# First loads in another queue order, and a new order of the work, in a fused attention and gated-FFN kernel

## The chip, the cores and the metric

The kernel runs on one core of a Trainium2 chip. The metric is the device time of one execution in microseconds (us): 387.93 us is the median of three runs of the kernel before (386.91 to 388.13).

## The reference, cut to what matters

```python
def phi(x):
    proj = np.einsum('bhsd,df->bhsf', x, w_phi)
    proj = proj - np.max(np.abs(proj), axis=-1, keepdims=True)
    return np.concatenate([np.exp(proj), np.exp(-proj)], axis=-1)
q_p, k_p = (phi(q), phi(k))
kv = np.einsum('bhsf,bhsd->bhfd', k_p, v)
z = np.sum(k_p, axis=2)
num = np.einsum('bhsf,bhfd->bhsd', q_p, kv)
den = np.einsum('bhsf,bhf->bhs', q_p, z)[..., None] + 1e-06
attn = num / den                      # 8 batches, 8 heads, 576 tokens, head size 64
x = attn.transpose(0, 2, 1, 3).reshape(4608, 512)
gate = np.maximum(x @ w_gate, 0.0)    # 512 x 1536
out = (gate * (x @ w_val)) @ w_out    # 1536 x 512
```

All inputs are float32. The kernel takes its matmuls in bf16.

## The kernel before, in words

Attention of eight batches feeds nine groups of a gated FFN. Of the 576 tokens of a batch, 512 are worked on as four chunks of 128; the other 64 are the "tails", which are taken together for two batches. FFN group g takes the 512 main tokens of batch g, and group 8 takes the tails of all batches.

The work is cut into small pieces, "atoms", each a few instructions on one or two engines, with a key. For batch b they are:

- k side, for each pair of heads u: `kT` (TensorE, PE in the profile, turns k by four transposing matmuls; batches 0 and 1 only, the others are turned by DMA), `kTc` (copy out of PSUM), `kr` (projection, L310), `km` (row maxima on VectorE, DVE, L317), `ke` (exponentials on ScalarE, ACT, L366), `kk` (factors `ek`, L377), `vs` (v times the factors, on GpSimd, POOL, or DVE, L326), `kv` (product of features and v, L447) and `kvc` (its copy, L455). Atoms with `u` in the key and `vsm` do the same for the tails.
- q side, for each half cp of the chunks: `qT` and `qTc` (turned as k is, eight transposes, L269 and L282), `qc` and `qr` (projections both ways), `qe` (exponentials, L504), `qm` (row maxima), `qk`, then `n` (numerators, L534), `nt` and `nu` (DVE, L553 and L565), `xu` (division, L574), and `xT` with `xc` (turning of the result, L269 and L594) or `xd` (the same by DMA).
- FFN group g: `fv` (value product and its copy by ACT or DVE, L665 and L680), `fg` (gate product and the DVE operation that joins both, L687) for 12 slices of 128 columns, and `fo` (output product, L713, copy, L723, store). Group 0 begins with 8 steps of half width (256 tokens), so that it can start when the first two chunks are there, and goes on with 8 of full width.

Nothing schedules these atoms at run time. The string `ORDER` lists their numbers, and `atoms.run` emits them in that order, so every engine's instruction stream and every DMA queue follows it; an engine executes its stream strictly in order. A prime behind a number puts that atom's copy or product on the other of two engines. `z5` emits five dummy matmuls on zeros (`keep_busy`, L193). PSUM is handed out in eight banks in turn.

Ahead of `ORDER` stand the first loads of batch 0, in float32: `w_phi` to `wf`, cast on DVE to `w2` (the profile's `w`); k into the buffer `vn1`, v into `vn0`; the tails into `km` and `vm`. POOL then copies one element of a loaded tile to `gate`, which holds back the loads behind it in POOL's stream (`ld` atoms: q, k of later batches and the weights, cast to bf16 on the way). v of later batches is loaded on SyncE's (SP's) queue.

## Time and profile before

| | |
|---|---|
| median of 3 runs | 387.93 us |
| the profiled execution's own time | 389.6 us |
| its span, first to last instruction | 387.8 us |
| PE busy | 368.0 us (95%) |
| DVE busy | 296.1 us (76%) |
| ACT busy | 217.9 us (56%) |
| POOL busy | 141.4 us (36%) |
| moved by DMA | 45.13 MB, mean 116 GB/s |

All times in the profile are counted from the start of the span. "Busy" is the time in which an engine executes something; the idle time before an instruction is put down to what released it. The granted clock is TensorE's own, as a share of full speed. A busy PE need not be at its peak, since ends of matmuls are modelled.

### The profile page before, as it was taken

The numbers are of one execution on the slowest core, as the hardware profiler recorded it, in microseconds if no ns is written. First come the engines' busy times: TensorE is split into PE (matmuls) and PEld (weight loads), VectorE is DVE, ScalarE is ACT, GpSimd is POOL, SyncE is SP. The second block draws the span as 40 slices with busy tenths as digits, with TensorE's granted clock in tenths as the row PEclk, the third lists the DMA queues.
The fourth block names the chain that finished last, engine by engine and source line by source line (L and its number), as shares of the span: only waits on it lengthen the run. The fifth ranks groups of instructions, "written<-read, shape, count | busy, mean of one in ns | idle before, by whom it ended". The sixth has DMA issues, their size and how long they took to land.

```text
span 387.8 us, 8651 instructions
## 1 busy us (share of the span) xinstructions
PE 368.0 (95%) x3316; PEld 198.1 (51%) x3365; DVE 296.1 (76%) x640; ACT 217.9 (56%) x509; POOL 141.4 (36%) x186
## 2 busy tenths in 40 slices
PE   4977999999999999999999999999999999999994
PEld 2556646544655555455546454555545544444441
DVE  2995987898898898999958998989777916932630
ACT  1994876569878835994694469664673112103110
POOL 2994383419288236181543235732210210000000
PEclk9998999999999999999999999999999999999999
DMA  7999995997859999993489716920310220011013
GB/s 180 210 239 187 175 179 87 181 210 98 136 83 135 181 189 139 189 203 57 141 158 234 125 41 128 159 56 2 96 54 2 43 96 27 15 54 54 2 27 82
DMA packets 91931, 45.13 MB, mean 116 GB/s; under 512 B 57970, under 2 KB 87282, under 8 KB 91890
## 3 DMA queue, kind: packets, MB, share of 16 engines
q1 hardware_dynamic: 62226, 30.22, 33.0%
q0 software_dynamic: 28256, 13.57, 31.9%
q10 hardware_dynamic: 1408, 0.79, 0.7%
q8 instruction: 26, 0.43, 0.5%
q14 instruction: 15, 0.12, 0.1%
HBM read 37.81 MB, written 9.44 MB: 122 GB/s over the span
## 4 chain that ended last, share of the span: by engine, by line
PE 85%; DMA 5%; DVE 4%; issue 2%; ACT 2%; POOL 1%; ACTq 0%; DVEq 0%; POOLq 0%
PE pa L665 46%; PE pa L713 23%; PE pa L534 5%; PE pa L447 5%; PE pa L310 4%; DMA qn<-in_q_dram 3%; PE pa L486 2%; DMA km<-in_k_dram 2%; PE pa L269 1%; ACT kp L366 1%; DVE mq L317 1%; DVE u L565 1%; DVE t L553 1%; DVE vs L423 0%; POOL vs L326 0%
## 5 line engine op out<-in xcount | busy, mean ns | idle before, releaser
L687 DVE SCALAR_TENSOR_TENSOR h<-pa,val_sb 128x512 bf16<-128x512 f32 (+1 forms) x112 | 74.1, 668 | 37.2 <-PE pa L665 29.0
L665 PE MATMUL pa<-xT,wg_sb 128*128 128x512 bf16 (+1 forms) x384 | 98.0, 371 | 1.2 <-DVE h L687 0.3
L665 PE MATMUL pa<-xT,wv_sb 128*128 128x512 bf16 (+1 forms) x386 | 98.0, 372 | 0.6
L713 PE MATMUL pa<-wo_sb,h 128*128 128x512 bf16 x415 | 97.0, 379 | 0.8 <-issue 0.2
L366 ACT ACTIVATE kp<-pa 128x512 bf16<-128x512 f32 (+1 forms) x148 | 76.9, 609 | 12.3 <-PE pa L310 8.7
L504 ACT ACTIVATE qp<-pa 128x512 bf16<-128x512 f32 x144 | 76.3, 631 | 12.3 <-PE pa L486 12.3
L680 ACT CAST val_sb<-pa 128x512 bf16<-128x512 f32 (+1 forms) x65 | 37.7, 580 | 72.6 <-PE pa L665 67.4
L326 POOL TENSOR_TENSOR vs<-vn,ek 128x512 bf16<-128x512 f32 x56 | 59.5, 1071 | 48.0 <-ACT ek L377 37.3
L574 POOL TENSOR_TENSOR xu<-u,r 128x512 bf16<-128x512 f32 x30 | 31.4, 1049 | 115.0 <-DVE r L572 79.4
L665 PEld LDWEIGHTS <-wv_sb 128*128 128x128 bf16 x448 | 42.0, 98 | 45.0 <-issue 0.7
L665 PEld LDWEIGHTS <-wg_sb 128*128 128x128 bf16 x448 | 41.9, 98 | 44.1 <-issue 0.7
L713 PEld LDWEIGHTS <-h 128*128 128x128 bf16 x432 | 39.8, 98 | 44.7 <-issue 1.2
L317 DVE TENSOR_REDUCE mk<-pa 128x4 f32<-128x512 f32 (+1 forms) x74 | 47.2, 667 | 6.0 <-PE pa L310 5.2
L317 DVE TENSOR_REDUCE mq<-pa 128x4 f32<-128x512 f32 x72 | 45.9, 681 | 4.0 <-PE pa L310 3.9
L553 DVE TENSOR_TENSOR t<-pa,cq 128x195 f32<-128x195 f32 (+3 forms) x120 | 38.1, 328 | 7.3 <-PE pa L534 4.8
L723 ACT COPY out_sb<-pa 128x512 f32<-128x512 f32 x26 | 15.6, 600 | 47.2 <-PE pa L713 40.9
L565 DVE TENSOR_TENSOR u<-pa,t 128x195 f32<-128x195 f32 (+3 forms) x120 | 38.4, 334 | 3.6
L534 PEld LDWEIGHTS <-qp 128*128 128x128 bf16 x640 | 28.5, 98 | 14.2 <-issue 1.7
L680 DVE CAST val_sb<-pa 128x512 bf16<-128x512 f32 (+1 forms) x47 | 31.1, 662 | 4.3 <-PE pa L665 3.5
L534 PE MATMUL pa<-kv,qp 128*128 128x65 bf16 x640 | 31.2, 194 | 1.1 <-ACT qp L504 0.9
L447 PEld LDWEIGHTS <-kp 128*128 128x128 bf16 x640 | 21.7, 97 | 5.5 <-ACT qp L504 0.9
L447 PE MATMUL pa<-vs,kp 128*128 128x65 bf16 x512 | 23.0, 193 | 1.3 <-ACT kp L366 0.5
(69 smaller groups left out, 266.8 us busy)
## 6 DMA issues: line engine op xcount, KB each, us to landing
out_dram<-out_sb SPq DMA_DIRECT2D x32, 256.0 KB, 2.5
vn<-in_v_dram SPq DMA_DIRECT2D x7, 1024.0 KB, 6.7
qn<-in_q_dram POOLq DMA_DIRECT2D x8, 512.0 KB, 8.2
kn<-in_k_dram POOLq DMA_DIRECT2D x7, 512.0 KB, 9.4
wv_sb<-in_moe_w_val_dram POOLq DMA_DIRECT2D x3, 512.0 KB, 10.9
wg_sb<-in_moe_w_gate_dram POOLq DMA_DIRECT2D x3, 512.0 KB, 12.2
...
vn<-in_k_dram SPq DMA_DIRECT2D x4, 256.0 KB, 5.1
```

The lines of the kernel that those rows point to most:

```text
L317: nc.vector.tensor_reduce(m, some.rearrange("p (c f) -> p c f", f=F), axis=AX.X, op=ALU.max, apply_absolute_value=True,)
L326: eng.tensor_tensor(dst[:, :, s, 0:D], src, ek[:, :, s : s + 1].to_broadcast(list(src.shape)), op=ALU.mult,)
L366: nc.scalar.activation(st["kp"][:, s, 0 : n // 2, par, :], st["banks"][par][:, 0 : n // 2 * F].rearrange("p (a f) -> p a f", f=F), AF.Exp, ...
L447: nc.tensor.matmul(kv_ps[:, hh, s, :], lhsT=lhsT, rhs=rhs, start=(n == 0), stop=(n == 19))
L504: nc.scalar.activation(x["qp"][:, s, slot].rearrange("p a b -> p (a b)"), st["cols", i][par], AF.Exp, scale=sign,)
L534: nc.tensor.matmul(pn[:, E * (2 * i + s) : E * (2 * i + s + 1)], lhsT=x["qp"][:, s, slot, blk, :], rhs=kvs[b, (lo + i) // 2][:, (lo + i) % ...
L553: nc.vector.tensor_tensor(x["t", j][rows, 0:n], ab[:, :, 1], c[:, :, None].to_broadcast([np_, n, E]), op=ALU.mult,)
L565: nc.vector.tensor_tensor(x["u"][rows, lo : lo + n], ab[:, :, 0], x["t", j][rows, 0:n], op=ALU.add)
L665: nc.tensor.matmul(ps, lhsT=w[:, dc, P * fi : P * fi + P], rhs=xTs[g][:, dc, lo:hi], start=(dc == 0), stop=(dc == NDC - 1),)
L680: copy_by(copy_of(alt, "ACT", "DVE"))(st["val", n], ps)
L687: nc.vector.scalar_tensor_tensor(st["h2"][:, fi, lo:hi], ps, 0.0, st["val", n], op0=ALU.max, op1=ALU.mult)
L713: nc.tensor.matmul(po, lhsT=st["h2"][:, fi, P * t : P * t + P], rhs=wo_sb[:, fi, c0:c1], start=(fi == 0), stop=(fi == NFC - 1),)
```

## The change

First the loads. Before, SP's queue took `w_phi`, k and v of two heads at a time, and ACT's queue the four tail loads. Now ACT's queue takes `w_phi` alone, and everything else goes to SP: k and v of heads 0 to 3 in turn, then k's tails, k of heads 4 to 7 in one DMA, v's tails, v of heads 4 to 7 in one DMA. The gate reads k of head 2 and no longer k's tails.

```diff
-    def heads_of(u):
-        return slice(2 * u, 2 * u + 2)
-
-    def load_first(name, src, eng, u):
-        load_main(0, name, src, eng, FP32, heads_of(u), buf="vn1" if name == "kn" else "vn0")
-
+    def load_first(name, src, lo, hi):
+        buf = "vn1" if name == "kn" else "vn0"
+        load_main(0, name, src, nc.sync, FP32, slice(lo, hi), buf=buf)
+
+    nc.scalar.dma_start(out=wf, in_=w_phi[None].to_broadcast([2, D, F]))
     inputs["kn", 0] = sb_in.tile([P, H, C, D], FP32, name="vn1")
-    nc.sync.dma_start(out=wf, in_=w_phi[None].to_broadcast([2, D, F]))
-    load_tails("km", k, 0, nc.scalar, FP32)
-    load_tails("vm", v, 0, nc.scalar, FP32)
-    load_first("kn", k, nc.sync, 0)
-    load_first("kn", k, nc.sync, 1)
-    load_first("vn", v, nc.sync, 0)
-    load_first("kn", k, nc.sync, 2)
-    load_first("vn", v, nc.sync, 1)
-    load_first("kn", k, nc.sync, 3)
-    load_first("vn", v, nc.sync, 2)
-    load_first("vn", v, nc.sync, 3)
+    load_first("kn", k, 0, 2)
+    load_first("vn", v, 0, 2)
+    load_first("kn", k, 2, 4)
+    load_first("vn", v, 2, 4)
+    load_tails("km", k, 0, nc.sync, FP32)
+    load_first("kn", k, 4, H)
+    load_tails("vm", v, 0, nc.sync, FP32)
+    load_first("vn", v, 4, H)
...
-    nc.gpsimd.tensor_copy(gate, inputs["km", 0][:, 0, 0:1])
+    nc.gpsimd.tensor_copy(gate, inputs["kn", 0][:, 2, 0, 0:1])
```

Then the whole `ORDER` is a new one, 13 dummy matmuls instead of 9 among it. Of its 62 lines, the first of each:

```diff
-ORDER = """z5 60 7 61' 104 62 64 65 8 116 105' 66 63 0 106 117 67 109 108 118 119 122 128 1 107 111 129 z2 130
...
+ORDER = """z5 104 105' z1 106 108 116 7 109 110 0 60 8 1 117 118 107 61 121 62 z2 128 140 63 111 113 112 120
...
```

By its key, the old one begins with `kT` of the tails (60) and loads q (7) and k of batch 1 (8) before the first weights (0); the new one begins with `kT` of heads 0 and 1 (104), and puts the first weights between q and k of batch 1.

SP's queue before, from its first row (`vn_104` holds k, `vn_114` v of batch 0; the last two rows are v of batch 1's tails and rows):

```order
L737 DMA wf<-in_w_phi_dram 128x1x128
L207 DMA vn_104<-in_k_dram 128x2x256 x2
L207 DMA vn_114<-in_v_dram 128x2x256
L207 DMA vn_104<-in_k_dram 128x2x256
L207 DMA vn_114<-in_v_dram 128x2x256
L207 DMA vn_104<-in_k_dram 128x2x256
L207 DMA vn_114<-in_v_dram 128x2x256 x2
L224 DMA vm<-in_v_dram 64x4x64 x2
L207 DMA vn_531<-in_v_dram 128x8x256
```

And now (`vn_105` holds k, `vn_107` v of batch 0):

```order
L207 DMA vn_105<-in_k_dram 128x2x256
L207 DMA vn_107<-in_v_dram 128x2x256
L207 DMA vn_105<-in_k_dram 128x2x256
L207 DMA vn_107<-in_v_dram 128x2x256
L224 DMA km_111<-in_k_dram 64x4x64 x2
L207 DMA vn_105<-in_k_dram 128x4x256
L224 DMA vm<-in_v_dram 64x4x64 x2
L207 DMA vn_107<-in_v_dram 128x4x256
L224 DMA vm<-in_v_dram 64x4x64 x2
L207 DMA vn_386<-in_v_dram 128x8x256
```

k's first rows now lead the queue, and the tails of k stand behind 1 MB of it.

DVE's stream before, from its first reduction to the copies of the turned q of batch 0 (`mk` are row maxima of k, 128x2 for the tails; the `tT` of 128x1024 are q):

```order
L317 TENSOR_REDUCE mk<-pa 128x2 x2
L282 COPY tT_184<-pa 128x512
L317 TENSOR_REDUCE mk<-pa 128x4 x3
L282 COPY tT_219<-pa 128x512
L317 TENSOR_REDUCE mk<-pa 128x4 x3
L282 COPY tT_265<-pa 128x512
L317 TENSOR_REDUCE mk<-pa 128x4 x2
L282 COPY tT_308<-pa 128x1024
L282 COPY tT_333<-pa 128x1024
```

And now:

```order
L317 TENSOR_REDUCE mk<-pa 128x4
L282 COPY tT_176<-pa 128x512
L317 TENSOR_REDUCE mk<-pa 128x4
L282 COPY tT_189<-pa 128x256
L317 TENSOR_REDUCE mk<-pa 128x4
L317 TENSOR_REDUCE mk<-pa 128x2
L317 TENSOR_REDUCE mk<-pa 128x4
L317 TENSOR_REDUCE mk<-pa 128x2
L282 COPY tT_239<-pa 128x512
L326 TENSOR_TENSOR vs<-vn_107,ek 128x8x64
L317 TENSOR_REDUCE mk<-pa 128x4 x4
L282 COPY tT_307<-pa 128x1024
```

One `vs` product (L326) has come to DVE, the copy of the tails (`tT_189`) too, and one copy of 128x512 has left it for ACT.

PE's stream before, from the turning of the first result chunk to the first FFN matmul (`xu` is the result, `qn` and `kn` are q and k of batch 1, L534 are numerators; the weight loads and repetitions are left out):

```order
L269 MATMUL pa<-ident_98,xu 128x128
...
L269 MATMUL pa<-ident_98,qn 128x128
...
L269 MATMUL pa<-ident_98,kn 128x128
...
L269 MATMUL pa<-ident_98,xu 128x128
...
L534 MATMUL pa<-kv,qp 128x65
...
L269 MATMUL pa<-ident_98,qn 128x128
...
L534 MATMUL pa<-kv,qp 128x65
...
L665 MATMUL pa<-xT,wv_sb 128x256
```

And now:

```order
L269 MATMUL pa<-ident_98,xu 128x128
...
L534 MATMUL pa<-kv,qp 128x65
...
L269 MATMUL pa<-ident_98,xu 128x128
...
L269 MATMUL pa<-ident_98,qn 128x128
...
L534 MATMUL pa<-kv,qp 128x65
...
L665 MATMUL pa<-xT,wv_sb 128x256
```

The first transpose of q of batch 1 used to stand ahead of four transposes of k, the turning of the second result chunk and ten numerator matmuls; now only the other eight transposes of q and four numerator matmuls stand between it and the FFN.

97 lines of the change are left out of this document (46 added, 51 removed), and 25 rows, old and new, of the table ORDER.

## Prediction

> **What bounds the kernel now.** I read the busy times first: PE is busy for 95% of the span. So the time is PE's work plus the gaps before and in it, and the next view is busy time by stretches (PE, PEld, DVE, ACT, POOL, then granted clock, DMA share, GB/s).
>
> ```profile
> 10.00:20.00 10.00, 8.92 (x101) 5.48 (x99) 9.18 (x16) 9.88 (x30) 9.25 (x16) 1.00 1.25 207
> 20.00:30.00 10.00, 7.72 (x160) 6.12 (x160) 9.29 (x28) 9.76 (x24) 9.66 (x14) 1.00 1.24 239
> 35.00:387.80 352.80, 343.71 (x3007) 181.25 (x3053) 273.02 (x585) 194.42 (x451) 118.41 (x148) 1.00 0.62 107
> 80.00:90.00 10.00, 9.37 (x75) 4.54 (x75) 9.45 (x19) 7.86 (x21) 4.42 (x6) 1.00 0.82 188
> 240.00:250.00 10.00, 9.50 (x116) 5.38 (x115) 9.63 (x19) 6.85 (x16) 8.96 (x12) 1.00 0.90 116
> 280.00:290.00 10.00, 9.49 (x100) 4.91 (x97) 7.54 (x14) 8.12 (x21) 1.09 (x1) 1.00 0.14 54
> 380.00:387.80 7.80, 2.77 (x13) 1.08 (x11) 0.69 (x1) 0.58 (x1) 0.00 (x0) 1.00 0.31 87
> ```
>
> From 35 us on PE lacks 352.80 - 343.71 = 9.1 us. Of these 5.0 lie at the very end (7.80 - 2.77: last copy and store, which the change leaves), 1.6 in the three stretches with a real gap, 2.4 in crumbs of some 0.1 in 10 us. A new order can win there 1.6 us at most, and lose as it pleases. From 10 to 30 us it is ACT, DVE and POOL that are full, and DMA moves over 200 GB/s. What ends this front is told by the chain of waits (start, length, what) and by PE's timeline.
>
> ```profile
> 1.49 5.92 DMA km<-in_k_dram
> 19.20 13.03 DMA qn<-in_q_dram
> ```
>
> ```profile
> 29.75 0.39 PE L269 MATMUL pa<-ident,xu 128*128 128x128 bf16 x4
> 32.28 0.62 PE L269 MATMUL pa<-ident,qn 128*128 128x128 bf16 x8 [2.14 <-DMA qn<-in_q_dram]
> 32.73 0.53 PE L269 MATMUL pa<-ident,kn 128*128 128x128 bf16 x4
> 33.06 0.63 PE L269 MATMUL pa<-ident,xu 128*128 128x128 bf16 x4
> 33.48 0.42 PE L534 MATMUL pa<-kv,qp 128*128 128x65 bf16 x4
> 33.72 1.04 PE L269 MATMUL pa<-ident,qn 128*128 128x128 bf16 x8
> 34.56 0.54 PE L534 MATMUL pa<-kv,qp 128*128 128x65 bf16 x6
> 34.91 1.04 PE L665 MATMUL pa<-xT,wv_sb 128*128 128x256 bf16 x4
> 36.43 0.60 PE L665 MATMUL pa<-xT,wv_sb 128*128 128x256 bf16 x4
> ```
>
> PE stands for 2.14 us until q of batch 1 lands, 13.0 us after its issue, and the FFN starts 2.63 us behind that landing (34.91 - 32.28). The stall costs more than itself: the last two rows are the same four matmuls, 1.04 and then 0.60. Stretches of 3.41 us show why:
>
> ```profile
> 26.11:29.52 3.41, 2.31 (x47) 1.80 (x46) 2.96 (x14) 3.40 (x7) 3.09 (x4) 1.00 1.26 254
> 29.52:32.94 3.42, 1.28 (x24) 1.08 (x22) 1.48 (x5) 1.07 (x2) 0.87 (x2) 0.98 1.24 209
> 32.94:36.35 3.41, 3.41 (x34) 3.03 (x32) 1.92 (x7) 1.96 (x4) 1.08 (x2) 0.51 1.38 201
> ```
>
> After a stretch with 1.28 us of matmuls the granted clock is 0.51 for 3.41 us; after one with 2.31 it stayed full. The point at which it falls lies between the two.
>
> **The change part by part.** *First loads.* Today k of heads 0 and 1 is issued at 1.51 and lands at 6.9 (1.51 + 5.4); the k tails release PE near 7.4 (1.49 + 5.92 in the chain).
>
> ```profile
> vn<-in_k_dram SPq DMA_DIRECT2D x1, 256.0 KB, 5.4
> 1.51 0.95 SPq L207 DMA_DIRECT2D vn<-in_k_dram  x2
> 2.00:3.00 1.00, 1.00 (x4) 0.15 (x1) 0.75 (x2) 0.00 (x0) 0.00 (x0) 1.00 0.26 64
> 3.00:4.00 1.00, 0.30 (x1) 0.00 (x0) 0.30 (x1) 0.29 (x1) 0.00 (x0) 1.00 0.91 262
> 4.00:5.00 1.00, 0.00 (x0) 0.00 (x0) 0.00 (x0) 0.99 (x1) 0.00 (x0) 1.00 1.14 213
> 5.00:6.00 1.00, 0.00 (x0) 0.00 (x0) 0.00 (x0) 0.00 (x0) 0.00 (x0) 1.00 1.14 258
> 7.55 0.19 POOL L754 COPY gate<-km 128x1 f32<-128x1 f32 x1 [5.90 <-DMA km<-in_k_dram]
> SPq L207 <- DMA km<-in_k_dram: 2.7, 1, 2.7
> ```
>
> Ahead of that k landing stand `w_phi`, k tails, most of the v tails and k itself, about 576 KB, which by these rows had been moved at 5.2; the landing is 1.7 later. Now only `w_phi` and k are ahead, 320 KB, moved at 4.0: I estimate a landing at 5.8. PE's first real work begins 1.7 us sooner. But the k tails now follow 1.2 MB: 2.6 + 1.2 MB at 240 GB/s + 1.7 = 9.4, and in the new order the projection of heads 2 and 3 stands behind their turning on PE. The gate opens with k of heads 2 and 3, estimated at 7.9, about where it opened (7.55). SP's queue waited 2.7 us for an earlier load before its fifth issue, so the new queue may pause too; 1 MB stands ahead there, which hides it.
>
> *Front work.* DVE's first reduction stood at 9.45; with k landed at 5.8 and 2.5 for turning, copy and projection (the tails took 2.0 from 7.4 to 9.45, and are half as wide) it stands near 8.3. Up to the copies of q, DVE gains a `vs` product (0.89) and the tails' copy (0.3, under half of a 128x512 one) and loses a copy of 0.69. Five dummies come ahead of q's transposes.
>
> ```profile
> 9.45 0.42 DVE L317 TENSOR_REDUCE mk<-pa 128x2 f32<-128x256 f32 x1 [3.16 <-PE pa L310]
> 18.05 1.28 DVE L282 COPY tT<-pa 128x1024 bf16<-128x1024 bf16 x2
> L326 DVE TENSOR_TENSOR vs<-vn,ek 128x512 bf16<-128x512 f32 x8 | 7.1, 891 | 1.4 <-ACT ek L377 1.3
> L282 DVE CAST tT<-pa 128x512 bf16<-128x512 f32 x3 | 2.1, 685 | 0.0
> 0.98 2.32 PE L193 MATMUL pa<-zeros 128*128 128x512 bf16 x5 [0.98 <-DVE zeros L748]
> 16.74 1.07 PE L269 MATMUL pa<-ident,qn 128*128 128x128 bf16 x16
> ```
>
> Five dummies cost 2.32 at half clock, and their cover is DVE, which reaches q's copies at 18.05 today and, by these gains and losses, at about the same time then. If PE is still at half clock there, the cover falls short by about 1 us. So the front's compute comes out between 1.1 early and 1.5 late; I take 0.5 late. Today compute stands ready at 30.1, 2.1 before q lands, so this is hidden.
>
> *q of batch 1.* On POOL's queue it is still the fifth of five 512 KB loads, behind q, first weights and k in another order; v of batch 1 follows on SP as before. DMA is full from 3 us to its landing, the bytes ahead are the same, so I leave it at 32.28, with 31.3 and 33.3 as bounds (the gate or that v up to 1 us apart). k of batch 1 goes behind one more 512 KB load, but its transposes now stand behind the last kv product of batch 0 and three numerator groups: hidden.
>
> *Behind q.* Four transposes of k, the four of the second result and one group of six numerators now stand ahead of the wait. Behind it: 16 transposes and four numerators. At full clock that is 1.07 (the row at 16.74) + 0.2 (half of the 0.42 at half clock) = 1.3 instead of 2.63: 1.4 us gained. Whether the clock is full: the stretch ahead of the landing then holds 1.28 plus these 14 matmuls (some 0.6 us at full clock) plus whatever the front comes late, so 1.9 to 2.9 where 1.28 was too little and 2.31 enough. I take full. Then the FFN work that ran from 34.91 to 36.35 at half clock gains 0.7 more. Together -2.1. The Trainium skill ("TensorE: Matmul & The Clock Gate", What's actually happening) has the clock fall after an idle window of about 3.4 us; here it fell after a window that held 1.28 us of work, so the trace is harsher. By the page's rule it would not fall in the changed kernel either, and the sum stays -2.1.
>
> *The rest of the order.* Value copies on DVE go from 47 to 39, output copies there from 10 to 13; both engines have time (DVE 273 of 353 us). I book +0.6 for the late front and for gaps of a new order, bounds -1.6 (all three gaps gone) and +1.7 (the second rival's extra work).
>
> Sum: -2.1 + 0.6 = -1.5. The profiled execution's own time of 389.6 (span 387.8, 1.8 around it) would be 388.1. It lies 1.67 above the median of the runs, so the median goes from 387.93 to **386.4**.
>
> **The rivals.**
>
> *The clock falls again.* The wait stays and the stretch before it stays too thin. Then the 14 matmuls gain only what they are worth at full clock, 0.55 us, and with 0.3 for the order the time is 387.7. For it: the two bounds leave the point open. Of the Trainium skill's same page, PE-mode transpose says that transposes do not count as PE-busy in the same way; eight of the 14 are transposes, so by it the stretch gains little and this rival wins. The trace gives some support: 3.24 us of matmuls from 9.04 to 12.46, many of them transposes, and the two dummies behind still take 0.5 each, as the five on the cold start did.
>
> ```profile
> 9.04:12.46 3.42, 3.24 (x29) 2.19 (x29) 2.65 (x5) 3.04 (x10) 3.35 (x6) 1.00 0.93 251
> 12.66 1.06 PE L193 MATMUL pa<-zeros 128*128 128x512 bf16 x2
> ```
>
> *DVE becomes the bound in group 0 (slower).* From the FFN's start to group 1, I count on DVE, new against old: two kv copies (0.42 each), a `vs` product (0.89), a q copy of 128x1024 (0.64 by the row at 18.05), a result copy and one `nu` (taken at 0.4 each) more; three value copies (two of half width, 0.4 each, one whole, 0.69) fewer: +1.7 us.
>
> ```profile
> L455 DVE CAST kv<-pa 128x260 bf16<-128x260 f32 x13 | 5.5, 421 | 1.3 <-PE pa L447 1.3
> L680 DVE CAST val_sb<-pa 128x512 bf16<-128x512 f32 x43 | 29.4, 685 | 4.3 <-PE pa L665 3.5
> 40.00:80.00 40.00, 39.63 (x417) 23.26 (x423) 34.74 (x80) 26.76 (x68) 18.11 (x26) 1.00 0.94 157
> ```
>
> DVE was busy 34.74 of 40 there. If PE starts earlier and at full clock, DVE has less time ahead of it and more to do; if it cannot use its free 5.3 us, the -2.1 is given back and the 1.7 come on top: 389.6. It decides when DVE is above 9.7 in 10 us from 35 to 75. Against it: those 5.3 us, and eight PSUM banks that let PE run ahead.
>
> *The loads do not land sooner.* All DMAs share the engines; if k lands at 6.9 as now while its tails land at 9.4 or later, the front is another 1.1 us late. With the 1.5 of its late bound and 0.6 for the 14 matmuls it ends 3.2 behind 30.1, which is 1.0 past q's landing: 387.4.
>
> **How the numbers follow.** Forecast (386.4, its own range 385.0 to 387.5) 0.40; clock falls (387.7) 0.20; DVE or another late engine (389.6) 0.32; late loads (387.4) 0.08. The range goes down to 384.7, the forecast with half the bounded gain in the later gaps and q 1 us sooner, and up to 389.9 to hold the slower case's middle. A measurement of this kernel tells 0.3% (1.2 us) from no change: faster means below 386.8, slower above 389.1. Faster: 0.36 of the forecast's 0.40 and 0.05 of the second case, 0.41. Slower: 0.26 of the third and 0.01 of the fourth, 0.27. The rest, 0.32, lies within.
>
> **What would show it.** Right: k's first transposes near 5.8; no stretch at half clock after 32; the first FFN matmul at 33.2 to 34; PE idle for 9 us or so in all from there on. Wrong in the front: that matmul later than 34.9, with q's landing past 33.3, or q's transposes waited for by ACT or DVE and not by DMA. Wrong in the order: waits of PE for DVE `h` or for `vs` above 0.5 us that are not there now. It would be wrong as a whole if compute, not q of batch 1, is what PE waits for at 32 us.

## The result and the profile after

The changed kernel takes 384.28 us (median of 20 runs, 383.72 to 388.33) against 387.56 us for the kernel before (20 runs, 386.17 to 390.45): ratio 0.9926, interval 0.9906 to 0.9946. That is 3.3 us faster, where 386.4 was predicted and 384.7 was the range's low end. The direction was right and the size was not. (The 387.93 us that the forecast started from is the median of the first three of the 20 runs of the kernel before.)

The profiled execution of the changed kernel took 387.17 us (span 385.4) and is one of its longer ones. A second profile of the same kernel, first experiment below, took 384.48 (span 382.7) and lies at the median, so both are read.

PE's timeline in the first profile (start, length, what, and in brackets the idle time ahead and what ended it): the first transposes of k, the first projection, then the end of the front.

```profile
3.63 1.09 PE L269 MATMUL pa<-ident,vn 128*128 128x128 f32 x4 [0.33 <-DMA vn<-in_k_dram]
6.28 0.40 PE L310 MATMUL pa<-w,tT 64*128 64x128 bf16 x8 [1.14 <-DVE w L751]
...
29.51 0.38 PE L269 MATMUL pa<-ident,xu 128*128 128x128 bf16 x4 [0.30 <-ACT xT L594]
31.37 1.07 PE L269 MATMUL pa<-ident,qn 128*128 128x128 bf16 x16 [1.48 <-DMA qn<-in_q_dram]
...
32.40 0.96 PE L665 MATMUL pa<-xT,wv_sb 128*128 128x256 bf16 x4
```

k of heads 0 and 1, issued at 0.73, frees PE at 3.63, and the next thing PE waits for is `w_phi`'s cast. The wait for q of batch 1 is still there, 1.48 instead of 2.14, but PE reaches it at 29.9 and the FFN starts 1.03 behind the landing, not 2.63. The stretches of 3.4 us (PE, PEld, DVE, ACT, POOL, granted clock, DMA share, GB/s) show that this execution lost the clock all the same:

```profile
29.10:32.50 3.40, 1.62 (x29) 1.36 (x26) 1.65 (x6) 0.97 (x3) 1.04 (x1) 1.00 1.24 216
32.50:35.95 3.45, 3.45 (x21) 2.51 (x18) 1.81 (x5) 1.64 (x3) 2.32 (x3) 0.51 0.81 107
```

The second profile, at the median, has the same order and another landing. Its PE rows, then the same stretches:

```profile
30.06 1.07 PE L269 MATMUL pa<-ident,qn 128*128 128x128 bf16 x16 [0.51 <-DMA qn<-in_q_dram]
...
31.09 0.60 PE L665 MATMUL pa<-xT,wv_sb 128*128 128x256 bf16 x4
```

```profile
29.10:32.50 3.40, 2.72 (x35) 2.27 (x35) 2.13 (x9) 1.89 (x4) 1.22 (x2) 1.00 1.21 227
32.50:36.00 3.50, 3.50 (x38) 3.09 (x37) 2.87 (x7) 1.38 (x4) 3.50 (x5) 1.00 1.15 146
```

q landed 1.3 sooner, PE had 2.72 us of work in the stretch, and the clock stayed. How early the front runs is told by three rows of DVE: its first reduction of k, its copy of the turned q of batch 0, and its first reciprocal, from which the first result follows. Of the kernel before the first two stand in the prediction (9.45 and 18.05); its reciprocal, and then the three rows of the first and of the second profile after:

```profile
27.30 0.19 DVE L572 RECIPROCAL r<-u 128x8 f32<-128x8 f32 x1
```

```profile
6.73 0.69 DVE L317 TENSOR_REDUCE mk<-pa 128x4 f32<-128x512 f32 x1 [0.51 <-PE pa L310]
...
17.32 1.29 DVE L282 COPY tT<-pa 128x1024 bf16<-128x1024 bf16 x2 [1.02 <-PE pa L269]
...
26.13 0.20 DVE L572 RECIPROCAL r<-u 128x8 f32<-128x8 f32 x1
```

```profile
7.20 0.69 DVE L317 TENSOR_REDUCE mk<-pa 128x4 f32<-128x512 f32 x1 [0.51 <-PE pa L310]
...
16.52 1.28 DVE L282 COPY tT<-pa 128x1024 bf16<-128x1024 bf16 x2
...
25.80 0.19 DVE L572 RECIPROCAL r<-u 128x8 f32<-128x8 f32 x1
```

| us | before | changed, first | changed, second |
|---|---|---|---|
| own time | 389.6 | 387.17 | 384.48 |
| DVE's first reduction | 9.45 | 6.73 | 7.20 |
| DVE copies q | 18.05 | 17.32 | 16.52 |
| DVE's first reciprocal | 27.30 | 26.13 | 25.80 |
| PE released by q of batch 1 | 32.28 | 31.37 | 30.06 |
| first FFN matmul | 34.91 | 32.40 | 31.09 |
| from there to the span's end | 352.9 | 353.0 | 351.6 |

Between the kernel before and the second profile, 389.6 - 384.48 = 5.1 us: q's landing 2.2 sooner, the FFN 1.6 closer behind it (2.63 to 1.03), 0.7 of FFN work that no longer runs at half clock, and a rest of 0.6 in all that comes later. The first profile lies 2.7 above the second: 1.3 by the later start of the FFN (32.40 and 31.09), 1.4 by FFN work at half clock (353.0 and 351.6). The medians are only 3.3 apart, because the profiled execution of before was one with a long wait for q, as the experiments show.

### The profile page after: what moved, and what is told of

Its sections match the earlier page's. It is cut to its first block, busy times and chain, and to the rows that moved or that the text cites. A ratio compares the mean times of both kernels' runs of the same rounds, so it can differ in the third digit from the quotient of the medians.

```text
span 385.4 us, 8644 instructions
## 1 busy us (share of the span) xinstructions
PE 367.2 (95%) x3319; PEld 197.0 (51%) x3369; DVE 294.3 (76%) x634; ACT 219.5 (57%) x510; POOL 146.0 (38%) x191
## 5 line engine op out<-in xcount | busy, mean ns | idle before, releaser
L665 PE MATMUL pa<-xT,wg_sb 128*128 128x512 bf16 (+1 forms) x386 | 99.3, 373 | 0.7
L665 PE MATMUL pa<-xT,wv_sb 128*128 128x512 bf16 (+1 forms) x385 | 99.1, 373 | 0.8
L680 ACT CAST val_sb<-pa 128x512 bf16<-128x512 f32 (+1 forms) x73 | 41.8, 572 | 82.4 <-PE pa L665 79.8
L366 ACT ACTIVATE kp<-pa 128x512 bf16<-128x512 f32 (+1 forms) x148 | 77.3, 609 | 13.3 <-PE pa L310 10.0
L326 POOL TENSOR_TENSOR vs<-vn,ek 128x512 bf16<-128x512 f32 x57 | 61.4, 1088 | 39.8 <-ACT ek L377 29.1
L723 ACT COPY out_sb<-pa 128x512 f32<-128x512 f32 x23 | 13.7, 594 | 42.0 <-PE pa L713 38.8
L534 PEld LDWEIGHTS <-qp 128*128 128x128 bf16 x640 | 27.9, 98 | 13.3 <-issue 1.4
L534 PE MATMUL pa<-kv,qp 128*128 128x65 bf16 x640 | 30.8, 193 | 0.7 <-ACT qp L504 0.7
L680 DVE CAST val_sb<-pa 128x512 bf16<-128x512 f32 (+1 forms) x39 | 26.3, 673 | 2.3 <-PE pa L665 0.9
L723 DVE COPY out_sb<-pa 128x512 f32<-128x512 f32 x13 | 8.9, 685 | 23.7 <-PE pa L713 23.6
## 6 DMA issues: line engine op xcount, KB each, us to landing
wv_sb<-in_moe_w_val_dram POOLq DMA_DIRECT2D x3, 512.0 KB, 10.5
```

The lines of the kernel that those rows point to most:

```text
L326: eng.tensor_tensor(dst[:, :, s, 0:D], src, ek[:, :, s : s + 1].to_broadcast(list(src.shape)), op=ALU.mult,)
L366: nc.scalar.activation(st["kp"][:, s, 0 : n // 2, par, :], st["banks"][par][:, 0 : n // 2 * F].rearrange("p (a f) -> p a f", f=F), AF.Exp, ...
L534: nc.tensor.matmul(pn[:, E * (2 * i + s) : E * (2 * i + s + 1)], lhsT=x["qp"][:, s, slot, blk, :], rhs=kvs[b, (lo + i) // 2][:, (lo + i) % ...
L665: nc.tensor.matmul(ps, lhsT=w[:, dc, P * fi : P * fi + P], rhs=xTs[g][:, dc, lo:hi], start=(dc == 0), stop=(dc == NDC - 1),)
L680: copy_by(copy_of(alt, "ACT", "DVE"))(st["val", n], ps)
```

## The experiments

My theory after the result: k's first rows on an empty queue, in an order that begins with them, bring the front's work forward on all engines, and the FFN's start with it. Rivals: it is only the clock that is no longer lost; it is the later part of the order; or it is the landing of q of batch 1. Times are medians, each with the ratio to the kernel before, measured beside it, and the interval of that ratio. The kernel before had another median each time (387.56 to 389.32); the changed kernel, measured three times, had 384.28, 384.35 and 384.35, with ratios from 0.9926 to 0.988. So a ratio tells whether a kernel differs from the kernel before, and variants of the changed kernel are better compared by their times.

### Which half of the change

**The changed kernel once more** (no edit).

> The changed kernel itself, for a second profile. Its first profile was one of its slower executions (387.2 us where the median is 384.3) and shows two stretches at half clock. Theory A (where the FFN starts): the first FFN matmul starts near 32.4 again and q of batch 1 lands near 31.4, whatever the clock does. Theory B (the clock): a profile near the median shows no half-clock stretch after 30 us, and the time beside the kernel before is 384.3 against 387.6. If this profile is near 384 and the clock falls all the same, theory B is wrong.

384.35 us (383.56 to 386.23, 12 runs), ratio 0.9911 (0.9883 to 0.9939); its profile is the second one above. Theory B held in it: no half clock after 30 us. Theory A gave 31.4 and 32.4 and had both too late by 1.3 (30.06 and 31.09). **The new loads alone** (shown against the changed kernel, whose order goes back to the old one):

```diff
-ORDER = """z5 104 105' z1 106 108 116 7 109 110 0 60 8 1 117 118 107 61 121 62 z2 128 140 63 111 113 112 120
+ORDER = """z5 60 7 61' 104 62 64 65 8 116 105' 66 63 0 106 117 67 109 108 118 119 122 128 1 107 111 129 z2 130
...
```

> The new loads under the old order. The old order begins with the tails of k, which now land near 8.8 instead of 7.4, so the front starts 1.3 us later; the gate opens 0.6 sooner, so q of batch 1 lands near 31.6. Theory A (the gain needs the new order, which works ahead of that wait): 387 to 388.5, no gain. Rival (the loads alone bring it, because q lands sooner): 386.7 or less.

388.05 us (387.18 to 391.07, 12 runs), ratio 1.0013 (0.9986 to 1.004): nothing gained. PE's rows:

```profile
9.07 0.66 PE L269 MATMUL pa<-ident,km 128*128 128x128 f32 x2 [5.77 <-DMA km<-in_k_dram]
...
31.91 0.61 PE L269 MATMUL pa<-ident,qn 128*128 128x128 bf16 x8 [0.25 <-ACT tT L282]
...
33.61 0.60 PE L665 MATMUL pa<-xT,wv_sb 128*128 128x256 bf16 x4
```

The old order begins with k's tails, which now stand behind 1 MB: PE starts at 9.07 and DVE's first reduction stands at 10.97. q of batch 1 is no longer waited for; the compute is, by ACT's copy. **The new order alone**, with the old loads (shown against the kernel before):

```diff
-ORDER = """z5 60 7 61' 104 62 64 65 8 116 105' 66 63 0 106 117 67 109 108 118 119 122 128 1 107 111 129 z2 130
+ORDER = """z5 104 105' z1 106 108 116 7 109 110 0 60 8 1 117 118 107 61 121 62 z2 128 140 63 111 113 112 120
...
```

> The new order under the old loads. Theory A: k of heads 0 and 1 lands at 6.9 instead of 3.6 and the front is 2 to 3 us later, q of batch 1 lands near 32.3; the FFN starts at 33.3 to 35, the time is 386 to 387.5, so about half of the gain is gone. Rival (the order's later part or the moved transposes bring it all): 384.3 to 385.

385.85 us (385.28 to 386.23, 12 runs), ratio 0.9955 (0.9933 to 0.9978): about half the gain.

```profile
6.20 1.09 PE L269 MATMUL pa<-ident,vn 128*128 128x128 f32 x4 [2.90 <-DMA vn<-in_k_dram]
...
30.82 1.06 PE L269 MATMUL pa<-ident,qn 128*128 128x128 bf16 x16
31.84 0.60 PE L665 MATMUL pa<-xT,wv_sb 128*128 128x256 bf16 x4
```

With the old loads k reaches PE at 6.20 and the FFN starts at 31.84, without any wait for q and sooner than the 33.3 that I had expected at the least. So the order gains by itself, and only under it do the loads add their 1.5 us (385.85 to 384.35). What the loads alone show is that they gain nothing of themselves: they must be met by an order that begins with what lands first.

### The clock

**The kernel before with eight dummy matmuls** ahead of its transposes of q of batch 1, so that PE has work while it waits:

```diff
-210 267' 208 230 231' 4 218 211 219 177 278 254 178' 220 189 190 255' 215 224 225 226 317 318' 221
+210 267' 208 230 231' 4 218 211 219 177 z8 278 254 178' 220 189 190 255' 215 224 225 226 317 318'
```

> The kernel before with eight more dummy matmuls (1.7 us at full clock) ahead of the first transposes of q of batch 1, inside the wait of 2.1 us. Theory B (the clock falls because the stretch before the landing is too empty): no half-clock stretch after 32 us, the first FFN matmul at 33.6 instead of 34.9, and 1.5 us faster than before: 386.1. If the clock fall costs nothing in the median: 387.6.

387.56 us (386.84 to 389.31, 12 runs), ratio 1.0009 (0.9983 to 1.0035).

```profile
30.04 1.89 PE L193 MATMUL pa<-zeros 128*128 128x512 bf16 x8 [0.25 <-ACT tT L282]
31.77 0.61 PE L269 MATMUL pa<-ident,qn 128*128 128x128 bf16 x8
...
33.43 0.60 PE L665 MATMUL pa<-xT,wv_sb 128*128 128x256 bf16 x4
```

The clock stayed at 1.00, but the dummies held PE until 31.77. In this execution q, issued at 18.86, had landed 11.3 us later, at 30.2, so they held PE up for some 1.5 us. In the median the cure costs what it saves, and theory B's 1.5 us did not come; three of the 12 runs still have a mean clock of 0.992 and take over 389. **The changed kernel with six dummies** at the same place:

```diff
-266 209 210 214 244 267' 211 206 207 177 178' 221 222 223 218 219 189 190' 317 208 215 220 278 279'
+209 210 214 244 267' 211 206 207 177 178' 221 222 223 218 219 189 190' z6 317 208 215 220 278 279'
```

> The changed kernel with six more dummy matmuls ahead of the transposes of q of batch 1, so that PE has work while it waits for that landing (computed results are the same). Theory H (some executions of the changed kernel still lose the clock behind that wait, as its first profile shows with 0.51 from 32.5 on, others don't): the clock stays full behind 32 us in all, the median is that of the better executions, 383.6 to 384.4, and the spread narrows to 1 us or so. Rival J (in most executions q lands with a wait too short to cost the clock; then the dummies only hold PE up): the first FFN matmul goes from 31.1 to 32 and the time to 385 to 385.5.

385.05 us (384.59 to 385.77, 6 runs), ratio 0.9932 (0.9906 to 0.9959). Rival J holds:

```profile
29.55 1.46 PE L193 MATMUL pa<-zeros 128*128 128x512 bf16 x6
30.84 1.06 PE L269 MATMUL pa<-ident,qn 128*128 128x128 bf16 x16
...
31.86 0.60 PE L665 MATMUL pa<-xT,wv_sb 128*128 128x256 bf16 x4
```

The FFN starts at 31.86. q, issued at 17.25, had landed 12.0 us later, ahead of the dummies, so these only held PE up, and the median is 0.7 above the changed kernel's. The spread is 1.2 us (384.59 to 385.77), as theory H had it; but of the changed kernel's 36 runs only five lie above 385.8, so six runs do not show that the long executions are gone. How often the kernel before loses the clock is told by the 35 runs of it that were taken with the first four experiments. One stretch of 3.41 us at 0.51 lowers the mean granted clock of the span by 3.41 x 0.49 / 386 = 0.0043. 16 runs had a mean of 0.997 or more, median 386.72; the 19 others, at 0.995 or less, had 388.46. So about half its executions lose it, and those are 1.7 us longer. That the clock is the whole of these 1.7 is not shown: the late landing that costs the clock is in them too. Nor does the mean tell where it was lost: the changed kernel's second profile ran at 0.50 from 8.1 to 14.9 and lies at the median all the same.

### The front of the order and its rest

Both orders were cut at the first FFN value product (`fv` of group 0) and crossed. **The old loads and front, with the new rest**, and **the new loads and front, with the old rest** (the edits are given in words, as the orders are long):

```diff
-old front | old rest        (the kernel before)
+old front | new rest
```

> Old loads and the old order up to the first FFN matmul, the new order from there on. In the profiles so far the span less the FFN's start is 352.3 and 352.6 us under the old order and 351.6 and 351.7 under the new one. Theory C (the later part of the new order is worth 0.7 us of its own): 387.3 beside 388.0. Rival (all of it is the front, the difference is noise of profiles): 388.0.

387.28 us (385.36 to 389.08, 12 runs), ratio 0.9945 (0.9917 to 0.9972).

```diff
-new front | new rest        (the changed kernel)
+new front | old rest
```

> New loads and the new order up to the first FFN matmul, the old order from there on: the other half of the same question. Theory C: 385.0 beside 384.35 for the changed kernel and 388.0 for the kernel before, span less FFN start 352.3. Rival: 384.35 and 351.6.

385.65 us (385.33 to 386.14, 6 runs), ratio 0.9917 (0.9889 to 0.9946). The rows of the one and then of the other:

```profile
30.25 0.62 PE L269 MATMUL pa<-ident,qn 128*128 128x128 bf16 x8 [0.61 <-DMA qn<-in_q_dram]
...
31.95 0.60 PE L665 MATMUL pa<-xT,wv_sb 128*128 128x256 bf16 x4
```

```profile
29.86 1.06 PE L269 MATMUL pa<-ident,qn 128*128 128x128 bf16 x16
30.88 0.60 PE L665 MATMUL pa<-xT,wv_sb 128*128 128x256 bf16 x4
```

The first profile matters for its landing: with the front and the loads of the kernel before, q of batch 1 released PE at 30.25, not at 32.28, after a wait of 0.61 and without a fall of the clock. This is the fastest of its 12 runs, so 30.25 is an early landing, as that of the profiled execution of before, 2 us above the median, is a late one. The second shows a gain of the front alone; from its first FFN matmul to its end it takes 353.3, where the profiles with the new rest take 351.3 to 351.7 (those of the first profile's half clock apart), and those of the old order without half clock 352.3 to 352.6. So in profiles of full clock the rest of the new order is worth 0.6 to 1.3 us behind the old front and 1.6 to 2.0 behind the new one; behind the new front the medians have 1.3 (385.65 here, 384.35 for the changed kernel). Behind the old front its gain is clear of noise (0.9945), but its size in the median is not settled, as the kernel before stood at 389.32 beside it. Busy times of PE behind the new front, with the old rest and with the new (this one from the kernel with a product back on POOL, below):

```profile
35.00:60.00 25.00, 24.56 (x259) 14.25 (x257) 22.57 (x43) 19.05 (x52) 15.53 (x24) 1.00 1.13 183
60.00:80.00 20.00, 19.43 (x211) 11.18 (x208) 17.07 (x49) 9.14 (x20) 4.01 (x4) 1.00 0.79 160
```

```profile
35.00:60.00 25.00, 25.00 (x286) 14.90 (x284) 23.30 (x47) 21.61 (x56) 14.80 (x23) 1.00 1.27 185
60.00:80.00 20.00, 20.00 (x186) 10.67 (x185) 17.70 (x51) 9.46 (x20) 4.01 (x4) 1.00 0.91 169
```

1.0 us of gaps lies here, in groups 0 and 1, where the prediction feared DVE. The new rest has none there in this profile. But the kernel before itself has 0.37 us of them between 35 and 80, and so has the changed kernel's second profile, so these gaps come with the mixture and are not what the rest gains over the kernel before. Most of that gain lies at the very end: from the start of ACT's last copy to the end of the span it is 4.7 to 5.0 us in the five profiles with the old rest, and 4.2 to 4.5 in the 15 with the new. In the second profile that is 0.5 of the 0.6.

### The landing of q of batch 1

**v of batch 1 later**: its 1 MB moves from SP's queue to POOL's, behind the second pair of weights.

```diff
-                lambda alt, b=b: load_main(b, "vn", v, nc.sync, FP32, buf=f"vn{b % 2}")
+                lambda alt, b=b: load_main(
+                    b, "vn", v, nc.gpsimd if b == 1 else nc.sync, FP32, buf=f"vn{b % 2}"
+                )
...
-153 191 192 147 161 163 10 160 162 155 30 165 154 159 126 127' 9 200 114 204 164 157 158 194 115
+153 191 192 147 161 163 10 160 162 155 30 165 154 159 126 127' 200 114 204 164 157 158 194 115 166
...
-199 2 230 197 173 174 182 183 201 175 3 29 185 186 176 187 242 243' 184 254 255 188 231 203 212 213
+2 230 197 173 174 182 183 201 175 3 29 185 186 9 176 187 242 243' 184 254 255 188 231 203 212 213
```

> The changed kernel with v of batch 1 (1 MB) on POOL's queue behind the second weights and the k tails of batch 1, no longer on SP's beside q of batch 1. Theory A (DMA is full and that v shares it with q): q lands 2 to 4 us sooner than 30.0 to 31.4, PE no longer waits for it, no execution loses the clock there; the FFN starts when the compute is ready, at 30.6 instead of 31.1, and the time is 383.6 to 384.0 with a narrower spread. Rival (q's landing is set by POOL's own queue): q lands as before, 384.35. If the second weights or v of batch 1 come too late, over 385.

383.99 us (383.63 to 384.44, 6 runs), ratio 0.9872 (0.9841 to 0.9904). The DMA issues of 16 to 22 us (KB, us to landing) of the changed kernel's second profile and of this one:

```profile
qn<-in_q_dram POOLq DMA_DIRECT2D x1, 512.0 KB, 12.5
```

```profile
qn<-in_q_dram POOLq DMA_DIRECT2D x1, 512.0 KB, 9.3
```

With the other queue's 1 MB gone from beside it, q lands at 17.73 + 9.3 = 27.0 and is never waited for; no run is above 384.44. In the 15 profiles with that load beside it, q took 9.7 to 13.3 us, in the five without, here and below, 8.5 to 9.7: the load seems to share its time with q, though the ranges touch. Without it the changed kernel's long executions are gone: none of the 28 runs of such kernels is above 384.5, while seven of the changed kernel's 36 are above 385. The median gains little. It was taken again with later experiments:

> The kernel of the late v of batch 1 once more, beside the other two: q of batch 1 lands near 27, no wait there, time 383.6 to 384.4 with a spread under 1 us. If the landing of q of batch 1 is no longer what sets the first FFN matmul of the changed kernel in its median execution (compute is ready at about the same time), it lies within 0.5 us of the changed kernel; if it still is, the gain is 1 us or more (383.2 or less).

383.82 us (383.50 to 384.08, 6 runs), ratio 0.990 (0.9875 to 0.9926), q 9.7 us under way: within 0.5 us of the changed kernel, so in a median execution q hardly sets the FFN's start any more.

### w_phi's queue

**`w_phi` first on SP's queue**, ahead of k, in the changed kernel:

```diff
-    nc.scalar.dma_start(out=wf, in_=w_phi[None].to_broadcast([2, D, F]))
+    nc.sync.dma_start(out=wf, in_=w_phi[None].to_broadcast([2, D, F]))
```

> The changed kernel with w_phi first on SP's queue instead of alone on ACT's. In the changed kernel k of heads 0 and 1 lands at 3.6 and PE then waits until 6.3 for w_phi, which lands near 6.0 as it did before. Theory D (on ACT's queue it is held up behind SP's four loads): first on SP it lands before 4.5, the first projection runs near 5.0, and the front is 0.3 to 1 us sooner: 383.4 to 384.1. Rival (its small pieces make it slow on any queue, or the k tails at 8.9 set the front): 384.35.

384.81 us (384.50 to 385.23, 6 runs), ratio 0.9895 (0.9867 to 0.9923).

```profile
6.19 1.09 PE L269 MATMUL pa<-ident,vn 128*128 128x128 f32 x4 [2.89 <-DMA vn<-in_k_dram]
...
7.96 0.61 PE L310 MATMUL pa<-w,tT 64*128 64x128 bf16 x8 [0.25 <-ACT tT L282]
```

64 KB of `w_phi` ahead of it on its own queue put k off by 2.4 us (6.19 for 3.77), 0.8 of it by a later issue (1.52 for 0.73), while `w_phi`'s cast came 1.05 sooner (5.42 for 6.47). The first projection is 1.2 later than in the changed kernel, and the FFN's start 0.2 (31.31). Theory D fell: the time is 0.5 above the changed kernel's. Alone on ACT's queue is the better place; why 1.2 us at the start cost only 0.2 at the end is told below.

### What ends the front: the gate, POOL, DVE or ACT

**The gate on k's tails again**, in the changed kernel:

```diff
-    nc.gpsimd.tensor_copy(gate, inputs["kn", 0][:, 2, 0, 0:1])
+    nc.gpsimd.tensor_copy(gate, inputs["km", 0][:, 0, 0:1])
```

> The changed kernel, but its gate reads k's tails again (which landed at 8.83 in it) and no longer k of head 2 (6.98), so POOL's queue of loads is held some 1.9 us longer. Theory F (q of batch 1 lands when the bytes ahead of it and beside it have been moved, DMA being full; the gate's time is lost in that): its landing stays between 30 and 31.5, first FFN matmul near 31.1, time 384.3, ratio 0.990. Theory G (the whole queue shifts with the gate, so the gate's new source is a part of the gain): q of batch 0 and q of batch 1 land some 1.9 later, PE waits 2 us or more for q of batch 1, the clock falls behind it, first FFN matmul near 33 and 0.7 more at half clock, time 386.5 to 387.5, ratio 0.996 to 0.999.

385.91 us (385.42 to 388.48, 12 runs), ratio 0.9951 (0.9925 to 0.9978). POOL's gate and PE's rows:

```profile
9.36 0.19 POOL L750 COPY gate<-km 128x1 f32<-128x1 f32 x1 [7.71 <-DMA km<-in_k_dram]
```

```profile
20.22 0.19 PE L447 MATMUL pa<-vsm,kp 128*128 128x65 bf16 x1 [0.87 <-POOL vsm L399]
23.36 0.28 PE L447 MATMUL pa<-vs,kp 128*128 128x65 bf16 x4 [1.12 <-POOL vs L423]
25.44 0.28 PE L447 MATMUL pa<-vs,kp 128*128 128x65 bf16 x4 [0.50 <-POOL vs L326]
...
31.57 1.06 PE L269 MATMUL pa<-ident,qn 128*128 128x128 bf16 x16
...
32.60 0.60 PE L665 MATMUL pa<-xT,wv_sb 128*128 128x256 bf16 x4
```

Theory F fell, and G held only in part: the front is 1.5 later, but not by q's landing, for which nobody waits. The gate stands in POOL's own stream, and with the gate 2.1 us later (9.36 for 7.22) the products of v come too late: PE waits three times for them, 2.5 us in all. That made me think that POOL's stream ends the front in the changed kernel as well, and that the product which the new order gives to DVE is a part of the gain. Three runs tested it. **That product back on POOL** in the changed kernel, and **that product alone on DVE** in the kernel before:

```diff
-122 64 119 123 125 65 66 129 130 141' 124' 67 69 132 133 142 145 143 134 144 131 135 146 z5 152 68
+122 64 119 123 125 65 66 129 130 141' 124 67 69 132 133 142 145 143 134 144 131 135 146 z5 152 68
```

> The changed kernel with one product of v and the factors of batch 0 (128x512, 1.04 us on POOL, 0.89 on DVE) back on POOL, as in the kernel before; nothing else is moved. Theory K (POOL's stream from the gate on is the front's bound): q of batch 1 is issued 1.0 later (18.6 instead of 17.54), POOL's first result product starts at 27.1 instead of 26.1 to 26.4, the first FFN matmul stands at 31.8 to 32.1, time 385.2 to 385.6, ratio 0.993. Rival L (DVE or ACT ends the front; the product on POOL costs nothing and DVE gains 0.9): first FFN matmul at 31.1 or earlier, time 384.3 or less, ratio 0.990 or less.

383.90 us (383.76 to 384.39, 6 runs), ratio 0.9871 (0.9831 to 0.9912). Theory K fell:

```profile
18.02 0.95 POOL L207 DMA_DIRECT2D qn<-in_q_dram  x1
```

```profile
29.52 1.06 PE L269 MATMUL pa<-ident,qn 128*128 128x128 bf16 x16
...
30.54 0.60 PE L665 MATMUL pa<-xT,wv_sb 128*128 128x256 bf16 x4
```

POOL issues q 0.5 later than in the changed kernel's second profile, and the FFN starts 0.55 sooner, since in this execution q had landed. The compute is neither later nor, with 0.7 us off DVE, sooner: DVE's copy of q stands 9.6 us behind its first reduction (9.3 there), its first reciprocal at 26.05 (25.80). So neither POOL's product nor DVE's 0.7 us ends the front by itself.

```diff
-121 69 113 110 123 112 124 120 131 133 135 140 68 141 z2 142 143 145 125 152 191 134 132 153 114 10
+121 69 113 110 123 112 124' 120 131 133 135 140 68 141 z2 142 143 145 125 152 191 134 132 153 114 10
```

> The kernel before with that one product moved from POOL to DVE and nothing else. Theory K: q of batch 1 is issued 1.0 earlier (18.0 to 18.2 instead of 18.9 to 19.2) and lands as much earlier, POOL's first result product starts about 26.5, the first FFN matmul stands 1 earlier than in the kernel before (33.4 to 33.9 instead of 34.9), time 386.5 to 387, ratio 0.996 to 0.998. Rival L: the product costs DVE 0.9 in a front that DVE ends, the first FFN matmul stands at 34.9 or later, time 388 to 389, ratio 1.000 to 1.003.

388.21 us (387.43 to 391.43, 12 runs), ratio 0.999 (0.996 to 1.002): in the median the move gains nothing. In its profile, the fastest of the 12, q is not waited for, but the compute is, and it is ready 1.3 later than in the kernel before (30.1); its DVE copies q at 18.62 instead of 18.05 and has its first reciprocal at 28.34 instead of 27.30. The profile also ran at 0.50 from 17.3 to 20.7, which may have a part in that. Rival L holds in the time; its first FFN matmul of 34.9 did not come (33.13), since q had landed:

```profile
31.43 0.61 PE L269 MATMUL pa<-ident,qn 128*128 128x128 bf16 x8 [0.25 <-ACT tT L282]
```

**The gate on k of head 0**, which lands first:

```diff
-    nc.gpsimd.tensor_copy(gate, inputs["kn", 0][:, 2, 0, 0:1])
+    nc.gpsimd.tensor_copy(gate, inputs["kn", 0][:, 0, 0, 0:1])
```

> The changed kernel with its gate on k of head 0, which landed at 3.6, no longer on head 2 (7.0 to 7.2); POOL's loads then start 3.4 us sooner, beside the first loads of SP's queue. Theory K in its plain form (front ends 19.2 after the gate) would put the first FFN matmul at 27.7 and the time at 381. I do not hold that form to be true so far down: the products wait for exponentials, whose first stood ready by 10.8, and k's later heads now share the engines with 2 MB more. Expected by theory K with that bound: POOL's first product at 10 to 10.8 with a wait ahead of it, q of batch 1 issued at 16.9 to 17.5, time 383.6 to 384.4. Rival M (the early loads take the engines from k of heads 2 to 7 and from the tails): their projections and the exponentials come 1 to 2 later, POOL waits for them, first FFN matmul at 32 or later, time 385.3 to 386.5.

385.74 us (384.40 to 387.31, 9 runs), ratio 0.9913 (0.9881 to 0.9946), 1.4 above the changed kernel. The profile is the slowest of the nine (387.31). The gate stands at 3.60. The load of k of heads 4 to 7 among the DMA issues of the first 9 us, and PE:

```profile
vn<-in_k_dram SPq DMA_DIRECT2D x1, 512.0 KB, 10.5
```

```profile
14.88 1.94 PE L269 MATMUL pa<-ident,vn 128*128 128x128 f32 x8 [2.85 <-DMA vn<-in_k_dram]
...
33.94 0.60 PE L665 MATMUL pa<-xT,wv_sb 128*128 128x256 bf16 x4
```

Rival M holds, and is larger than I gave it: with POOL's loads beside them k of heads 4 to 7 takes 10.5 us instead of 6.1 in the changed kernel's second profile, and PE waits 2.85 for it. Of the three places tried, the one between is the best: late enough for k, early enough for POOL's products.

**Both small gains together** (the late v and the product on POOL; each by itself was 0.3 to 0.5 below the changed kernel, not measured beside it), and now beside the changed kernel:

```diff
-122 64 119 123 125 65 66 129 130 141' 124' 67 69 132 133 142 145 143 134 144 131 135 146 z5 152 68
+122 64 119 123 125 65 66 129 130 141' 124 67 69 132 133 142 145 143 134 144 131 135 146 z5 152 68
...
+                    b, "vn", v, nc.gpsimd if b == 1 else nc.sync, FP32, buf=f"vn{b % 2}"
```

> The late v of batch 1 and the product back on POOL, both. Theory N (the front is DVE's: from its copy of the turned q to its first reciprocal 9.3 us, then 4.6 to the first FFN matmul where q of batch 1 has landed; each of the two edits only takes away the rest of a wait for that landing): first FFN matmul at 30.4 to 30.9, time 383.6 to 384.0, no better than either. Rival O (they add up, as DVE is also freed of 0.7 us): first FFN matmul at 29.8 to 30.2, time 383.2 to 383.5.

384.10 us (383.95 to 384.39, 4 runs), ratio 0.9875 (0.9833 to 0.9917), first FFN matmul at 30.78. And the changed kernel:

> The changed kernel itself once more, beside the other: 384.0 to 384.6, first FFN matmul between 30.5 and 32.4 as the landing of q of batch 1 has it (29 to 31.4).

384.35 us (383.95 to 384.69, 4 runs), ratio 0.988 (0.9844 to 0.9915), first FFN matmul at 31.33. They don't add up, which theory N foretold, though with the product off DVE it gives no reason for DVE's 9.7 us from its copy of q to its reciprocal. ACT was left: it is busy for all of 18 to 28 us in the changed kernel. **One copy off ACT** (the turned k of heads 6 and 7 to DVE), on the base of both small gains, and then **a second one** (`kvc` of heads 4 and 5):

```diff
-122 64 119 123 125 65 66 129 130 141' 124 67 69 132 133 142 145 143 134 144 131 135 146 z5 152 68
+122 64 119 123 125 65 66 129 130 141 124 67 69 132 133 142 145 143 134 144 131 135 146 z5 152 68
```

> The kernel with the late v and the product back on POOL, and the copy of the turned k of heads 6 and 7 (128x512, 0.65 us on ACT, 0.69 on DVE) on DVE instead of ACT. Theory P (ACT's stream, full from its first exponentials of k to its last ones of q, ends the front): ACT's first exponentials of q stand 0.5 to 0.65 sooner (17.8 to 18.1 instead of 18.4 to 18.7), the first FFN matmul at 30.0 to 30.4 instead of 30.78, time 383.3 to 383.7. Rival N (DVE ends it): its first reciprocal comes 0.4 to 0.7 later than the 26.30 of the base, first FFN matmul at 31.1 to 31.5, time 384.5 to 384.8.

383.95 us (383.69 to 384.31, 6 runs), ratio 0.9899 (0.9862 to 0.9937), first FFN matmul at 30.69 instead of 30.78.

```diff
-202 136 137 138 198 193 156 179 196 139 167 195 149 148 150 205 151 168 180 169 170 171 181 172 199
+202 136 137 138 198 193 156 179 196 139' 167 195 149 148 150 205 151 168 180 169 170 171 181 172 199
```

> The same, and one copy of kv (128x260, 0.45 us) moved from ACT to DVE as well. Theory P: another 0.3 to 0.5 off, as long as DVE has the time, first FFN matmul at 29.6 to 30.1, time 383.0 to 383.5. If DVE is then as late as ACT, no more than with one copy (30.0 to 30.4). Rival N: later still, 31.4 to 32, time 384.8 to 385.3.

384.11 us (383.95 to 384.46, 6 runs), ratio 0.9904 (0.987 to 0.9938), first FFN matmul at 30.87. Theory P fell too, and N with it: with 0.65 us off ACT and 0.69 on DVE the front ends 0.1 sooner. The rows of ACT and of PE in the first of the two show where the time went:

```profile
24.34 0.38 ACT L457 CAST kv<-pa 128x260 bf16<-128x260 f32 x1 [0.27 <-PE pa L449]
```

```profile
23.53 0.28 PE L449 MATMUL pa<-vs,kp 128*128 128x65 bf16 x4 [0.44 <-POOL vs L328]
```

ACT now waits 0.27 for PE's kv product, where it had no such wait on the base, and that product 0.44 for POOL's `vs` (0.24 on the base). (Lines are two higher in this kernel.) So no one engine was found that ends the front. It looks as if ACT, DVE and POOL ran side by side and handed work to each other, so that what is taken off one is waited for at the next; only this pair of rows shows it. What did move the front is when it begins. DVE's marks through the runs:

| us | first reduction | copy of q | first reciprocal | first FFN matmul |
|---|---|---|---|---|
| new loads, old order | 10.97 | 19.58 | 28.82 | 33.61 |
| old loads and front, new rest | 9.15 | 17.55 | 26.84 | 31.95 |
| old loads, new order | 8.64 | 17.96 | 27.22 | 31.84 |
| `w_phi` first on SP | 8.63 | 17.31 | 26.71 | 31.31 |
| changed kernel, third profile | 7.67 | 17.44 | 26.71 | 31.33 |
| both small gains | 7.53 | 16.56 | 26.30 | 30.78 |
| product back on POOL | 7.09 | 16.67 | 26.05 | 30.54 |
| gate on k of head 0 | 7.95 | 20.31 | 29.32 | 33.94 |

Where q of batch 1 has landed, the FFN starts 4.5 to 4.8 us behind the first reciprocal, in the old order as in the new (so the moved matmuls save time mainly where PE waits for q), and the reciprocal 8.8 to 9.8 behind the copy of q (11.4 with the gate on the tails). Of the first reduction's 2.2 us between the kernel before and the changed one's second profile, 1.5 arrive at the reciprocal; with `w_phi` first on SP, whose first reduction is 1.4 later, 0.9 of it arrives there, and at the FFN only 0.2, because the changed kernel's profile waited 0.5 for q and this one did not. The tie is loose: the changed kernel's third profile begins 1.0 sooner than the one with `w_phi` on SP and has its reciprocal at the same 26.71, and with the gate moved either way the front begins early and ends late (7.95 and 29.32; on the tails 7.32 and 28.11). An early beginning helps and does not suffice; what holds the front from there on stays open.

## Why the prediction was wrong

Two terms of the sum failed. q's landing was left at 32.28, a term of nothing, with the front taken as 0.5 late and hidden behind it; q came at 31.37 and 30.06, and the front was 0.6 to 1.5 early. And +0.6 was booked for a late front and for new gaps, where the rest of the order gained 0.6 or more.

*The first loads.* The mechanism was right and its size wrong. k was put at 5.8 by the bytes ahead of it; it freed PE at 3.63, because `w_phi`, on the other queue, is not ahead of it at all: only with `w_phi` on the same queue did it come near the estimate (6.19). DVE's first reduction was put at 8.3 and stood at 6.73, 7.20 and 7.67 in three profiles, held there by `w_phi`'s cast. The tails' landing was put at 9.4 and freed PE at 8.8 and 8.9.

*The front work.* Here the prediction failed first. It added `vs`, the tails' copy and the dummies to DVE and took the front's compute as 0.5 late, within 1.1 early and 1.5 late. By DVE's reciprocal it was 0.6 to 1.5 early (27.30 to 26.71, 26.13 and 25.80 in three profiles), or up to 0.5 less beside two other profiles of the old front (26.84 and 26.95). The sum of the added work was about right: 9.3 us from the first reduction to the copy of q instead of 8.6, 0.7 more where 0.5 was counted. But it starts 1.8 to 2.7 us sooner and not 1.2, and there is no sign of the 1 us by which the dummies were to hold DVE up: in the second profile DVE copies q at 16.52 without a wait, and the wait of 1.02 in the first is not theirs, as its dummies were done at 15.5 and PE stood 1.13 for q of batch 0.

*q of batch 1.* Held at 32.28, with 31.3 as the early bound, since DMA is full and the bytes ahead are the same. It released PE at 31.37 and 30.06; in the product's run and the third of the changed kernel PE took it up without a wait at 29.52 and 30.30. Its issue is 1.2 to 1.7 sooner (POOL's stream reaches it at 17.54 to 18.04, not at 19.20), and its landing scatters: 11.4 to 13.3 us behind the issue in the changed kernel's three profiles. Taking one execution's landing as the kernel's was the mistake; with the same front and loads another profile had it at 30.25. The prediction's last sign of being wrong as a whole, that PE waits for compute and not for q, came in the changed kernel's third profile and not in its first two.

*Behind q.* 1.4 was predicted for the shorter way to the FFN; 2.63 became 1.03, so 1.6. But most of it is the clock: the old order, where the clock stayed full, takes 1.70 and 1.66 (31.91 to 33.61 and 31.77 to 33.43), so the 14 moved matmuls are worth 0.65 and the clock the rest.

*The clock.* "I take full" is right in the second and third profile and wrong in the first: a stretch with 1.62 us of matmuls was followed by 0.51, as 1.28 was before. 2.31 and more kept it. Another stretch of the first profile, 15.43 to 18.84, four such lengths ahead of the fall, held 1.94 and kept it too, so the point lies between 1.62 and 1.94. Transposes count at least in part, against the rival's second ground: that stretch held 1.07 us of them and 0.87 of other matmuls, while one with 0.69 and the same 0.87 was followed by 0.50 (13.93 to 17.34 of the kernel before with the product on DVE). The Trainium skill ("TensorE: Matmul & The Clock Gate", What's actually happening) has the clock fall after an idle window; if any work keeps a window from being idle, there would have been no fall with 1.62 us of work in it, and the trace disagrees. The rival that the clock falls again is what the first profile shows; its price, however, was less than the landing brought.

*The rest of the order.* The term that decided: +0.6 was booked for the late front and for new gaps, with -1.6 as the lower bound. There was no late front, and the rest of the order gained 0.6 to 1.3, within the bound, 0.5 of it at the last copy and store, which the prediction held unchanged. With the right sizes the sum for the profiled execution would be -2.2 (q) - 1.6 - 0.7 - 0.6 = -5.1, which is what the second profile has; the -1.5 had the two negative terms behind q right and lacked the other two.

*From the execution to the median.* The prediction moved its sum unchanged to a median that lay 1.67 lower. This step hid an error of the opposite sign: what that execution had lost more than the median, a late q, is just what the change takes away, so of the 5.1 the median could gain only 3.3.

*The rivals.* DVE did not become the bound in group 0: in the profile shown PE is busy for all of 35 to 80 us with the new rest, and in the second profile it lacks 0.37 there, as before. That the loads don't land sooner was wrong by 3.3 us for k (6.9 there, 3.63 measured).

## What to carry to other kernels

New loads and the order that uses them are one change: the same loads gained nothing under an order that began with the tile that they had put behind 1 MB. Where a stall is the largest number of a profile, take a second execution before pricing it: a landing that scatters by 2 us makes the profiled one a poor base, and what it lost beyond the median can't be won at the median. A gate that holds back loads sits in its engine's stream, so it also holds back the compute behind it: here both an earlier and a later one cost 1.4 to 1.6 us.
